# Low halves, range check and first reads of a float64 MLP's weights, moved between engines and queues

## The chip, the cores and the metric

The kernel runs on one core of a Trainium2 chip. The metric is the device time of one execution in microseconds. The kernel before took 887.0 us (median of 3 runs, 886.07 to 888.24). The execution that the profiler recorded took 887.57 us, of which 885.9 us are the span of its instructions.

Engines are named as the profile does: PE is TensorE's matmuls and PEld its weight loads, DVE is VectorE, ACT is ScalarE, POOL is GpSimd, SP is SyncE, whose queue (SPq) issues nearly all transfers.

## The reference, cut to what matters

Three stages work on 3072 tokens of 384 features. A gated linear attention (4 sequences of 768 positions, 8 heads of 48) feeds a dense MLP, and that feeds a mixture of 8 experts in which each token goes to one.

```
f = 1 / (1 + exp(-f_logit))
state = f[t] * state + outer(k[t], v[t]);  y[t] = q[t] @ state      # attention
h = x @ w_in;  x2 = (h * sigmoid(h)) @ w_out                        # first MLP: 384 -> 2048 -> 384
e = argmax(x2 @ w_gate);  out = p[e] * relu(x2 @ w1[e]) @ w2[e]     # 8 experts: 384 -> 1024 -> 384
```

The MLP's two matrices arrive as float64 (8 bytes a value), everything else as float32. So w_in and w_out are 6.3 MB each, and the kernel has to make float32 values of them before it can use them.

## The kernel before, in words

Tokens are cut into 24 chunks of 128. Chunks go through the attention in six steps (`att0` to `att5`), and through the MLP in 9 groups of 2 or 3 chunks. For each group and each of the 16 tiles of 128 hidden features there is a slot: `moe_h` makes the tile's hidden values (`ph` in PSUM), ACT takes a tanh (`se`), DVE multiplies (`sg`), ACT rounds that to a high half (`gh`), and a subtraction gives the low half (`gl`). `moe_o` of that tile comes two slots later (LAG = 2) and adds to the group's output (`px`). Every product is three matmuls: high by high, high by low, low by high. The 144 slots go: group 0 tiles 0 to 7 (slots 0 to 7), group 1 all 16 tiles (slots 8 to 23), group 0 tiles 8 to 15 (slots 24 to 31), and then group by group, with 384 columns in place of 256. After the last slot come the experts.

The weights of the MLP are made in 32 pieces of 384 KB (16 of w_in, 16 of w_out), each needed from its tile's slot on in group 1, half of them already in group 0. For a piece, SP reads the raw words into a buffer (`in_raw`, `out_raw`; pool `raw`, 2 buffers; a w_in piece takes two transfers, a w_out piece one). `narrow` then makes float32 bits of them with three DVE instructions: a TENSOR_SCALAR (line 288) and two SCALAR_TENSOR_TENSOR (lines 291 and 294) into `in_cv` or `out_cv`. A fourth DVE instruction, the TENSOR_REDUCE of line 249, takes the least magnitude of the raw high words into `wmin`; at the end of the run that decides whether a slower, general version must follow. ACT then rounds to the high half (`in_hi`, `out_hi`, line 225), and POOL subtracts (`in_lo`, `out_lo`, line 226). Instructions that are pinned in program order are shown at a helper's line, 198.

Which instruction follows which is laid down when the program is built. A table gives each step a slot, a scheduler may move instructions on an engine as far as their data allow, and the order of TensorE's matmuls and of what is pinned stays as written. On the chip each engine takes its list in order, and an instruction that waits holds up all behind it. The transfers of a queue also start in order, and a new one must find one of 8 completion semaphores free.

Other names that the rows show: `kt` and `qt` are the turned keys and queries of a chunk (`att2`), `am` the masked scores, `a_all` the chunk's decay (written to DRAM as `ends` and read back), `state` the running state, `xs` the table of 4096 rows from which the experts read, filled first with a constant by 8 transfers of 776 KB (`prefill`, from a row in the tile `big`).

Of the kernel before, what the change touches and what calls it, by code (L numbers as in the profile page):

```python
# [9 lines left out]
F32 = mybir.dt.float32  # L10
# [11 lines left out]
P = 128  # L22
CAP = 512
ROW = 388
# [11 lines left out]
STP = (1, 2, 3, 4, 5, 6, 7)  # L36
PI = 12
PO = 12
CX = 0
LF = -27  # L40
LV = -16
CL = 32
ND = 1
MO = 'oeh'
TAIL = 'TooflfmfpfrffwgfkfftF'
# [9 lines left out]
ST6 = (14, 17, 19, 21, 23, 25)  # L55
LD = (-30, -30, -10, -5, -3, 5, 11)
LFD = ()
WP = ()
S1 = (-2, 1, 3, 5, 6, 8)
ASH = 3  # L60
SG = 2
# [14 lines left out]
PRD = 2  # L76
PU = 1
PD = 2
LOV = (8, 8)
FMIN = -44.0  # L80
LMIN = -43.9
ST = ST0, ST1, ST2, ST3, ST4, ST5, ST6
# [9 lines left out]
def kernel(  # L92
# [14 lines left out]
    nc = tc.nc  # L107
    B, H, S, D = q.shape
    NT, DM = out.shape
    DFF = moe_w_in.shape[1]  # L110
    E, _, F2 = moe2_w1.shape
    KC = DM // P
    NF = DFF // P
# [18 lines left out]
    main = ExitStack()  # L132
    ps = main.enter_context(tc.tile_pool(name="ps", bufs=1, space=PSUM))
    wts = main.enter_context(tc.tile_pool(name="wts", bufs=16))
    raw = main.enter_context(tc.tile_pool(name="raw", bufs=2))
    phase = ExitStack()
    att = phase.enter_context(tc.tile_pool(name="att", bufs=1))
    late = phase.enter_context(tc.tile_pool(name="late", bufs=1))
# [21 lines left out]
    wgc = const.tile([P, KC, E], F32, name="wgc")  # L160
    big = late.tile([P, 6 * 512], F32R, tag="big", name="big")
    xt0 = [big[:, i * 2 * DM : (i + 1) * 2 * DM].rearrange("p (r c t) -> p r c t", r=2, c=KC) for i in range(2)]
    extra = [big[:, 4 * DM + ROW + i * DM : 4 * DM + ROW + (i + 1) * DM].bitcast(U32) for i in range(2)]
    zrow = big[:, 4 * DM : 4 * DM + ROW].bitcast(F32)
    BANKS = {0: "haahhaaa", 1: "haahhaaa"}

# [30 lines left out]
    def keep(fn):  # L197
        return lambda *a, **k: tc.keep_in_program_order(fn(*a, **k))

    def new_unit(key):  # L200
        kind = key[0]
        full = [P, 4, KC, P] if kind in ("in", "w1") else [P, 4, DM]
        nm = "_".join(str(x) for x in key)
        units[key] = tuple(wts.tile(full, F32R, tag="wt", name=f"{nm}_{x}") for x in ("hi", "lo"))

    def part_of(src, kind, i, n):
        cols = slice(i * P, (i + n) * P)
        return (src[:, cols] if kind in ("in", "w1") else src[cols, :]).rearrange("(c p) f -> p c f", p=P)

    def load_raw(t, src, kind, i):  # L210
        cols = slice(i * P, (i + 1) * P)
        if kind == "out":
            view = lambda a: a[cols, :]
        else:
            view = lambda a: a[:, cols]
        x = view(src).bitcast(U32)
        if kind == "out":
            nc.sync.dma_start(out=t, in_=x.rearrange("(c p) f -> p c f", p=P))
            return
        nc.sync.dma_start(out=t[:96], in_=x[: KC * 96].rearrange("(c p) f -> p c f", c=KC))  # L220
        nc.sync.dma_start(out=t[96:], in_=x[KC * 96 :].rearrange("(c p) f -> p c f", c=KC))

    def split(key, h, x, lo_engine):
        hi, lo = units[key]
        (keep(nc.scalar.copy) if key == ("w1", 1, 1) and RT > 1 else nc.scalar.copy)(hi[:, h], x)  # L225
        lo_engine.tensor_sub(lo[:, h], x, hi[:, h].bitcast(F32))  # L226

    def load_piece(kind, i):
        u, h = divmod(i, 4)
        src = moe_w_in if kind == "in" else moe_w_out  # L230
        nm = f"{kind}_{i}"
        if h == 0:
            new_unit((kind, u))
        shape = [P, KC, P] if kind == "in" else [P, 1, DM]
        if src.dtype == I64:
            t = raw.tile(shape + [2], U32, tag="raw", name=f"{nm}_raw")
            load_raw(t.rearrange("p c f w -> p c (f w)"), src, kind, i)
            made = len(pieces_made)
            pieces_made.append(i)
            if made % (2 + CX) < CX and made < CL:  # L240
                x = extra[made % (2 + CX)]
                x = x.rearrange("p (c f) -> p c f", c=shape[1])
            else:
                x = raw.tile([P, ROW], U32, tag="cv", name=f"{nm}_cv", bufs=2)[:, :DM].rearrange("p (c f) -> p c f", c=shape[1])
            t2 = t.rearrange("p c f w -> p (c f) w")
            pin = keep if i < (PI if kind == "in" else PO) else lambda fn: fn
            narrow(t2, x.rearrange("p c f -> p (c f)"), pin)
            j = i if kind == "in" else NF + i
            pin((nc.gpsimd if made in WP else nc.vector).tensor_reduce)(
                out=wmin[:, j : j + 1], in_=t2[:, :, 1].bitcast(F32), axis=AX.X, op=ALU.min, apply_absolute_value=True  # L250
            )
            x = x.bitcast(F32)
        else:
            x = raw.tile(shape, F32, tag="raw", name=f"{nm}_raw")
            nc.sync.dma_start(out=x, in_=part_of(src, kind, i, 1))
        split((kind, u), h, x if kind == "in" else x[:, 0], nc.gpsimd)

    pieces_made = []
    halves = {}
# [91 lines left out]
    def att2(n):  # L351
        pq = use(n, 1, f"pq_{n}")
        for r in range(NPR):
            pe.transpose(
                pq[:112, r * P : (r + 1) * P],
                qpads[n % 2][:, 2 * r : 2 * r + 2, :].rearrange("p h d -> p (h d)")[:, :112],
                ident,
            )
        pk = use(n, 2, f"pk_{n}")
        for r in range(NPR):  # L360
            pe.transpose(
                pk[:112, r * P : (r + 1) * P],
                kpads[n % 2][:, 2 * r : 2 * r + 2, :].rearrange("p h d -> p (h d)")[:, :112],
                ident,
            )
        pq3 = pq[:112, :].rearrange("p (r t) -> p r t", r=NPR)
        pk3 = pk[:112, :].rearrange("p (r t) -> p r t", r=NPR)
        kt = att.tile([112, NPR, P], F32, tag="kt", name=f"kt_{n}", bufs=2)
        qt = att.tile([112, NPR, P], F32, tag="qt", name=f"qt_{n}", bufs=2)
        nc.scalar.copy(qt, pq3)  # L370
        nc.vector.tensor_copy(kt, pk3)
        bd[n] = (kt, qt)

    def att3(n):
# [117 lines left out]
    def moe_g(g, i):  # L492
# [4 lines left out]
        (nc.scalar.copy if g < GACT else nc.vector.tensor_copy)(hi, t)  # L497
        (nc.gpsimd if (g, i) < LOV else nc.vector).tensor_sub(lo, t, hi.bitcast(F32))  # L498
        gt[g, i] = (hi, lo)
# [554 lines left out]
    wmin = const.tile([P, 32], F32, name="wmin")  # L1054
# [28 lines left out]
    def at(slot, fn, *args):  # L1083
        plan.setdefault(slot, []).append((fn, args))
# [24 lines left out]
    for u in range(4):  # L1109
        for h in range(4):  # L1110
            at(UI[4 * u + h], load_piece, "in", 4 * u + h)
            at(UO[4 * u + h], load_piece, "out", 4 * u + h)
    for g in range(NG - 1):
        s0 = {0: L0, 1: L1}.get(g, pos[g, NF - 1] + LAG + 1)
        for t in range(sizes[g]):
            at(s0 + t, flip_rows, g, t)
            at_end(s0 + t, gate, g, t)
        s0 += sizes[g]
        at(s0, pick, g)
        at(s0 + RD, route, g)  # L1120
# [119 lines left out]
```

## Time and profile before

| | |
|---|---|
| median of 3 runs | 887.0 us |
| profiled execution | 887.57 us, span 885.9 us |
| PE busy | 837.0 us (94%) |
| DVE busy | 432.1 us (49%) |
| ACT busy | 380.6 us (43%) |
| POOL busy | 344.5 us (39%) |
| PE's wait behind an instruction of another engine, 0 to 150 us | at most 7.7 us for one cause |

How to read it: a windows row gives for a stretch the busy time of each engine with the count of instructions, then the mean clock granted to TensorE (1.00 is 2.4 GHz, 0.50 is 1.2 GHz), the busy share of the 16 DMA engines (the records of packets overlap, so it can come out above 1), and GB/s. In the timeline the bracket is the engine's idle time before the instruction and what ended it.

### The profile page before, as it was taken

How to read it: one execution, taken by the hardware profiler on the slowest of the kernel's cores; microseconds unless marked ns; L12 is line 12 of the kernel's file. 1: busy time of each engine (PE TensorE's matmuls, PEld its weight loads, DVE VectorE, ACT ScalarE, POOL GpSimd, SP SyncE). 2: the span in 40 equal slices, each digit the busy share in tenths (PEclk: the TensorE clock that was granted, in tenths of full speed). 3: DMA queues.
4: the chain of work that ended last, by engine and by line, in shares of the span. 5: the costliest groups of instructions: out<-in, count | busy, mean ns of one | idle time of the engine just before them, and what ended most of it. 6: DMA issues, size and time to landing. Idle time of an engine off the chain costs nothing. (4 is left out here: it accounts for less than half of the span.)

```text
span 885.9 us, 15549 instructions
## 1 busy us (share of the span) xinstructions
PE 837.0 (94%) x5684; PEld 796.0 (90%) x5684; DVE 432.1 (49%) x1040; ACT 380.6 (43%) x796; POOL 344.5 (39%) x361
## 2 busy tenths in 40 slices
PE   7779888999999999999999999999999999999994
PEld 4678778998999999999999999998898999999994
DVE  5889876355444345344335434333545355345520
ACT  5443443435345445345345343354444354345420
POOL 6565745443535525544544533445500100110011
PEclk9769979999999999999999999999899999999998
DMA  9654539231122313213212310213246344445500
GB/s 157 148 134 121 139 115 305 65 64 37 58 43 55 80 21 63 65 35 60 69 32 44 75 24 19 72 37 117 92 142 197 130 127 153 136 131 186 161 28 27
DMA packets 157479, 83.38 MB, mean 94 GB/s; under 512 B 114924, under 2 KB 153053, under 8 KB 157392
## 3 DMA queue, kind: packets, MB, share of 16 engines
q1 hardware_dynamic: 154112, 72.79, 31.7%
q0 software_dynamic: 3280, 9.49, 2.9%
q8 instruction: 47, 0.77, 0.4%
q14 instruction: 40, 0.33, 0.1%
HBM read 63.03 MB, written 16.33 MB: 90 GB/s over the span
## 5 line engine op out<-in xcount | busy, mean ns | idle before, releaser
L498 POOL TENSOR_TENSOR gl<-sg,gh 128x384 fp32r<-128x384 f32 (+1 forms) x136 | 133.2, 980 | 193.7 <-ACT gh L497 191.4
L489 DVE SCALAR_TENSOR_TENSOR sg<-se,ph 128x384 f32<-128x384 f32 (+1 forms) x144 | 73.0, 507 | 205.6 <-ACT se L487 193.0
L323 PE MATMUL px<-out_lo,gh 128*128 128x384 f32 x384 | 138.1, 360 | 1.0 <-ACT x L532 0.8
L487 ACT ACTIVATE se<-ph 128x384 f32<-128x384 f32 (+1 forms) x144 | 65.2, 453 | 167.9 <-PE ph L323 158.5
L323 PE MATMUL px<-out_hi,gl 128*128 128x384 f32 x384 | 132.1, 344 | 5.2 <-POOL gl L498 5.1
L323 PE MATMUL px<-out_hi,gh 128*128 128x384 f32 x384 | 131.4, 342 | 0.0
L323 PE MATMUL ph<-xtl,in_hi 128*128 128x384 f32 (+1 forms) x384 | 128.1, 334 | 1.2 <-POOL xtl L461 0.6
L323 PE MATMUL ph<-xth,in_hi 128*128 128x384 f32 (+1 forms) x384 | 125.5, 327 | 0.0
L323 PE MATMUL ph<-xth,in_lo 128*128 128x384 f32 (+1 forms) x384 | 125.4, 327 | 0.0
L497 ACT CAST gh<-sg 128x384 fp32r<-128x384 f32 (+1 forms) x144 | 68.6, 476 | 72.6 <-DVE sg L489 71.2
L766 POOL DMA_INDIRECT out_dram<-o,oi x25 | 24.1, 962 | 178.7 <-DVE w_lo L226 112.4
L225 ACT CAST w_hi<-w_raw 128x384 fp32r<-128x384 f32 x124 | 57.4, 512 | 56.6 <-DMA w_raw<-in_moe_w_dram 54.7
L323 PEld LDWEIGHTS px<-out_hi,gl 128*128 128x128 f32 x384 | 73.8, 192 | 6.7 <-POOL gl L498 6.0
L323 PEld LDWEIGHTS ph<-xtl,in_hi 128*128 128x128 f32 x384 | 73.9, 193 | 3.8 <-POOL xtl L461 2.5
L323 PEld LDWEIGHTS px<-out_lo,gh 128*128 128x128 f32 x384 | 73.5, 192 | 3.7 <-ACT x L532 1.1
L323 PEld LDWEIGHTS ph<-xth,in_lo 128*128 128x128 f32 x384 | 74.1, 193 | 0.0
L323 PEld LDWEIGHTS ph<-xth,in_hi 128*128 128x128 f32 x384 | 73.9, 192 | 0.0
L323 PEld LDWEIGHTS px<-out_hi,gh 128*128 128x128 f32 x384 | 73.6, 192 | 0.0
L226 DVE TENSOR_TENSOR w_lo<-w_raw,w_hi 128x384 fp32r<-128x384 f32 x104 | 53.5, 554 | 35.9 <-ACT w_hi L225 35.6
L323 PE MATMUL po<-w_lo,hh 128*128 128x384 f32 (+6 forms) x200 | 67.8, 339 | 0.0
L323 PE MATMUL po<-w_hi,hh 128*128 128x384 f32 (+6 forms) x200 | 67.3, 336 | 0.0
L323 PE MATMUL po<-w_hi,hl 128*128 128x384 f32 (+6 forms) x200 | 67.3, 336 | 0.0
(240 smaller groups left out, 1692.6 us busy)
## 6 DMA issues: line engine op xcount, KB each, us to landing
w_raw<-in_moe_w_dram SPq DMA_DIRECT2D x64, 384.0 KB
xs<-big SPq DMA_DIRECT2D x8, 776.0 KB
out_raw<-in_moe_w_out_dram SPq DMA_DIRECT2D x16, 384.0 KB
xe<-xs SPq DMA_DIRECT2D x7, 776.0 KB
f<-in_f_logit_dram SPq DMA_DIRECT2D x24, 192.0 KB
k<-in_k_dram SPq DMA_DIRECT2D x24, 192.0 KB
q<-in_q_dram SPq DMA_DIRECT2D x24, 192.0 KB
v<-in_v_dram SPq DMA_DIRECT2D x24, 192.0 KB
```

Source lines behind the costliest of these rows:

```text
L225: (keep(nc.scalar.copy) if key == ("w1", 1, 1) and RT > 1 else nc.scalar.copy)(hi[:, h], x)
L226: lo_engine.tensor_sub(lo[:, h], x, hi[:, h].bitcast(F32))
L323: ins = nc.tensor.matmul(*a, **k)
L487: nc.scalar.activation(e, ph[:, :GT], AF.Tanh, scale=0.5)
L489: nc.vector.scalar_tensor_tensor(out=t, in0=e, scalar=1.0, in1=ph[:, :GT], op0=ALU.add, op1=ALU.mult)
L497: (nc.scalar.copy if g < GACT else nc.vector.tensor_copy)(hi, t)
L498: (nc.gpsimd if (g, i) < LOV else nc.vector).tensor_sub(lo, t, hi.bitcast(F32))
L766: nc.gpsimd.indirect_dma_start(out=out[:, :], out_offset=bass.IndirectOffsetOnAxis(ap=idx[:n], axis=0), in_=o[:n], in_offset=None, bounds_ ...
```

## The change

For the MLP's float64 weights:

- the low half is subtracted on DVE in place of POOL (32 instructions);
- the range check no longer stands with the piece. Each piece is read from DRAM a second time (`verify_piece`, tiles `in_again`, `out_again`), and DVE's TENSOR_REDUCE works on that copy. The table places these from slot 44 on, one every 2.5 slots;
- the pool of raw buffers has 4 buffers, which second reads share;
- the first 4 pieces (5 transfers) are read from ACT's queue, the others from SP's.

Two more edits: the copy of the turned keys (`kt`) of chunks 0 to 6 goes from DVE to ACT, and the low half of the hidden values (`gl`) is made on POOL for groups 0 and 1 alone (32 instructions); for the 104 of groups 2 to 8 that POOL made, it goes to DVE.

```
-LOV = (8, 8)
+LOV = (2, 0)
+RAW = 4
+VS = 44
+VD = 5
+KACT = 7
-    raw = main.enter_context(tc.tile_pool(name="raw", bufs=2))
+    raw = main.enter_context(tc.tile_pool(name="raw", bufs=4))
...
-            load_raw(t.rearrange("p c f w -> p c (f w)"), src, kind, i)
...
+            load_raw(t.rearrange("p c f w -> p c (f w)"), src, kind, i, nc.scalar if made < RAW else nc.sync)
...
-            j = i if kind == "in" else NF + i
-            pin((nc.gpsimd if made in WP else nc.vector).tensor_reduce)(
-                out=wmin[:, j : j + 1], in_=t2[:, :, 1].bitcast(F32), axis=AX.X, op=ALU.min, apply_absolute_value=True
-            )
...
-        split((kind, u), h, x if kind == "in" else x[:, 0], nc.gpsimd)
+        split((kind, u), h, x if kind == "in" else x[:, 0], nc.vector)
+
+    def verify_piece(kind, i):
+        src = moe_w_in if kind == "in" else moe_w_out
+        if src.dtype != I64:
+            return
+        shape = [P, KC, P] if kind == "in" else [P, 1, DM]
+        t = raw.tile(shape + [2], U32, tag="raw", name=f"{kind}_{i}_again")
+        load_raw(t.rearrange("p c f w -> p c (f w)"), src, kind, i, nc.sync)
+        j = i if kind == "in" else NF + i
+        nc.vector.tensor_reduce(
+            out=wmin[:, j : j + 1], in_=t.rearrange("p c f w -> p (c f) w")[:, :, 1].bitcast(F32), axis=AX.X,
+            op=ALU.min, apply_absolute_value=True,
+        )
...
-        nc.vector.tensor_copy(kt, pk3)
+        (nc.scalar.copy if n < KACT else nc.vector.tensor_copy)(kt, pk3)
...
+    for j in range(2 * NF):
+        at(VS + j * VD // 2, verify_piece, ("in", "out")[j % 2], j // 2)
```

The order of TensorE's instructions is the same in both programs. Two places differ in a way that matters below. The first is SP's queue at the end of the weights' reads. In a name such as `out_13_raw`, 13 is the tile; `v_6`, `q_7`, `k_7` and `ends` belong to chunks 6 and 7. Before:

```order
L218 DMA out_13_raw_1374<-in_moe_w_out_dram 128x768
L218 DMA out_14_raw_1430<-in_moe_w_out_dram 128x768
L344 DMA ends_75<-ep_6_1420 1x384
L192 DMA k_7_1709<-in_k_dram 128x8x48
L192 DMA q_7_1707<-in_q_dram 128x8x48
L346 DMA a_all_84<-ends_75 48x4x1 x2
L218 DMA out_15_raw_1469<-in_moe_w_out_dram 128x768
L1134 DMA xs_76<-big_91 128x4x388 x8
L192 DMA v_7_1740<-in_v_dram 128x8x48
```

And now, at the same place of SP's queue:

```order
L1141 DMA xs_76<-big_91 128x4x388 x8
L218 DMA out_13_raw_1345<-in_moe_w_out_dram 128x768
L192 DMA v_6_1176<-in_v_dram 128x8x48
L218 DMA out_14_raw_1400<-in_moe_w_out_dram 128x768
L218 DMA out_15_raw_1438<-in_moe_w_out_dram 128x768
L220 DMA in_0_again_2523<-in_moe_w_in_dram 96x3x256
L221 DMA in_0_again_2523<-in_moe_w_in_dram 32x3x256
L349 DMA ends_75<-ep_6_1390 1x384
L192 DMA q_7_1675<-in_q_dram 128x8x48
L192 DMA k_7_1677<-in_k_dram 128x8x48
L218 DMA out_0_again_2666<-in_moe_w_out_dram 128x768
L351 DMA a_all_84<-ends_75 48x4x1 x2
```

The 8 transfers of the prefill stood behind the last piece of weights; they now stand ahead of the last three pieces, of `v_6` and of chunk 6's `ends`, and the second reads follow.

The second place is DVE's list from slot 21 on (`sg_1_13` is group 1, tile 13, slot 21; `sg_0_8` is slot 24). Before:

```order
L489 SCALAR_TENSOR_TENSOR sg_1_13_1562<-se_1_13_1560,ph_1_13_1550 128x256
L390 TENSOR_TENSOR am_6_0_1574<-sc_6_0_1564,trir_78 128x512
L390 TENSOR_TENSOR am_6_1_1576<-sc_6_1_1565,trir_78 128x512
L489 SCALAR_TENSOR_TENSOR sg_1_14_1600<-se_1_14_1598,ph_1_14_1588 128x256
L489 SCALAR_TENSOR_TENSOR sg_1_15_1624<-se_1_15_1622,ph_1_15_1612 128x256
L446 TENSOR_TENSOR state_85<-pu_6_1638,a_all_84 48x4x48 x2
L489 SCALAR_TENSOR_TENSOR sg_0_8_1671<-se_0_8_1669,ph_0_8_1659 128x256
```

And now, the first part of the same place:

```order
L494 SCALAR_TENSOR_TENSOR sg_1_13_1530<-se_1_13_1528,ph_1_13_1518 128x256
L395 TENSOR_TENSOR am_6_0_1542<-sc_6_0_1532,trir_78 128x512
L395 TENSOR_TENSOR am_6_1_1544<-sc_6_1_1533,trir_78 128x512
L293 TENSOR_SCALAR out_13_cv_1347<-out_13_raw_1345 128x384
L296 SCALAR_TENSOR_TENSOR out_13_cv_1347<-out_13_raw_1345,out_13_cv_1347 128x384
L494 SCALAR_TENSOR_TENSOR sg_1_14_1568<-se_1_14_1566,ph_1_14_1556 128x256
```

And further on, from the first of the second reads to slot 25's product (`sg_0_9`):

```order
L258 TENSOR_REDUCE wmin_96<-in_0_again_2523 128x1
L299 SCALAR_TENSOR_TENSOR out_15_cv_1440<-out_15_raw_1438,out_15_cv_1440 128x384
L226 TENSOR_TENSOR out_3_lo_1273<-out_14_cv_1402,out_3_hi_1272 128x384
L226 TENSOR_TENSOR out_3_lo_1273<-out_15_cv_1440,out_3_hi_1272 128x384
L494 SCALAR_TENSOR_TENSOR sg_0_8_1639<-se_0_8_1637,ph_0_8_1627 128x256
L258 TENSOR_REDUCE wmin_96<-out_0_again_2666 128x1
L451 TENSOR_TENSOR state_85<-pu_6_1606,a_all_84 48x4x48 x2
L494 SCALAR_TENSOR_TENSOR sg_0_9_1663<-se_0_9_1661,ph_0_9_1651 128x256
```

The narrowing of tile 13 of w_out now stands between the products of slots 21 and 22, and reduces of second reads stand among the products from slot 24 on. Although the table places them from slot 44, 28 of the 32 stand ahead of slot 36's product (`sg` of group 2, tile 4), and the other 4 ahead of slot 39's.

## Rows read from the trace of the kernel before

**Rows 1.** Windows by stretch: us, busy by engine (count), TensorE clock, DMA share, GB/s.
```profile
20.00:40.00 20.00, 14.03 (x104) 12.00 (x101) 17.14 (x30) 7.45 (x15) 13.35 (x11) 0.78 0.66 156
40.00:60.00 20.00, 14.92 (x76) 13.93 (x75) 17.27 (x29) 11.09 (x19) 10.32 (x11) 0.59 0.40 113
...
80.00:100.00 20.00, 19.04 (x159) 17.83 (x158) 17.77 (x38) 8.82 (x23) 13.06 (x16) 1.00 0.51 136
...
300.00:400.00 100.00, 99.22 (x756) 95.38 (x752) 43.88 (x110) 43.13 (x84) 43.98 (x41) 1.00 0.23 49
```
**Rows 2.** Waits of TensorE, 0 to 150: us in total, times, longest.
```profile
PE pq L328 <- DVE qpad L343: 7.7, 3, 3.9
...
PE ph L323 <- POOL in_lo L226: 3.1, 1, 3.1
```
**Rows 3.** Windows, 14 to 145: all; L226; tile wmin; L291; L294; tile kt.
```profile
14.00:145.00 131.00, 107.55 (x733) 99.67 (x733) 114.08 (x203) 59.43 (x128) 79.98 (x78) 0.80 0.55 141
...
14.00:145.00 131.00, 0.00 (x0) 34.92 (x32) 0.80 0.55 141
...
14.00:145.00 131.00, 17.38 (x32) 0.00 (x0) 0.80 0.55 141
...
14.00:145.00 131.00, 24.46 (x32) 0.80 0.55 141
...
14.00:145.00 131.00, 22.48 (x32) 0.80 0.55 141
...
14.00:145.00 131.00, 8.13 (x112) 6.82 (x112) 4.08 (x6) 0.80 0.55 141
```
**Rows 4.** Lines L294 and L198's reduce, 14 to 145: ns min/median/max, first and last start.
```profile
L294 DVE SCALAR_TENSOR_TENSOR out_cv<-out_raw,out_cv x16: 543/762/1240, 17.8 to 142.7; 128x384 uint32<-128x384 uint32 x16
...
L198 DVE TENSOR_REDUCE wmin<-out_raw x12: 539/541/546, 18.2 to 112.8; 128x1 f32<-128x384 f32 x12
```
**Rows 5.** Groups of VectorE by form, 14 to 145: busy, mean ns, idle before.
```profile
L198 DVE TENSOR_SCALAR out_cv<-out_raw 128x384 uint32<-128x384 uint32 x12 | 9.0, 753 | 0.8 <-DMA out_raw<-in_moe_w_out_dram 0.8
...
L198 DVE TENSOR_SCALAR in_cv<-in_raw 128x384 uint32<-128x384 uint32 x12 | 8.3, 694 | 2.3 <-DMA in_raw<-in_moe_w_in_dram 1.4 <-POOL in_lo L226 0.9
```
**Rows 6.** Timeline of VectorE: start, us, what, [idle before <- releaser].
```profile
36.79 0.42 DVE L489 SCALAR_TENSOR_TENSOR sg<-se,ph 128x256 f32<-128x256 f32 x1 [1.81 <-ACT se L487]
...
41.56 0.35 DVE L198 TENSOR_SCALAR in_cv<-in_raw 128x384 uint32<-128x384 uint32 x1
...
116.46 0.42 DVE L489 SCALAR_TENSOR_TENSOR sg<-se,ph 128x256 f32<-128x256 f32 x1 [0.81 <-ACT se L487]
...
125.54 0.36 DVE L288 TENSOR_SCALAR out_cv<-out_raw 128x384 uint32<-128x384 uint32 x1 [2.21 <-DMA out_raw<-in_moe_w_out_dram]
...
152.98 0.42 DVE L489 SCALAR_TENSOR_TENSOR sg<-se,ph 128x256 f32<-128x256 f32 x1 [2.11 <-ACT se L487]
...
187.55 0.55 DVE L489 SCALAR_TENSOR_TENSOR sg<-se,ph 128x384 f32<-128x384 f32 x1
```
**Rows 7.** Page, parts 5 and 6: low halves of the late weights; prefill of the slots.
```profile
L226 DVE TENSOR_TENSOR w_lo<-w_raw,w_hi 128x384 fp32r<-128x384 f32 x104 | 53.5, 554 | 35.9 <-ACT w_hi L225 35.6
...
xs<-big SPq DMA_DIRECT2D x8, 776.0 KB
```
**Rows 8.** Windows: small loads at the start; one w_in read; the prefill.
```profile
0.00:5.00 5.00, 2.74 (x6) 0.73 (x6) 2.24 (x4) 1.32 (x2) 4.34 (x30) 1.00 0.65 125
...
118.00:120.00 2.00, 2.00 (x9) 1.90 (x9) 2.00 (x4) 0.00 (x0) 1.13 (x2) 0.50 0.61 195
...
146.00:148.00 2.00, 2.00 (x18) 2.00 (x16) 0.42 (x1) 0.68 (x3) 0.76 (x2) 1.00 1.05 367
```
**Rows 9.** Timeline of SyncE's queue: reads of the raw weights.
```profile
110.42 0.33 SPq L220 DMA_DIRECT2D in_raw<-in_moe_w_in_dram  x1
...
122.30 0.35 SPq L218 DMA_DIRECT2D out_raw<-in_moe_w_out_dram  x1
...
127.45 4.98 SPq L218 DMA_DIRECT2D out_raw<-in_moe_w_out_dram  x2
```

More of the change, by code (lines that the diff above doesn't have):

```diff
@@ L38 @@
 PO = 12
-CX = 0
 LF = -27
 LV = -16
-CL = 32
+KACT = 7
 ND = 1
@@ L57 @@
 LFD = ()
-WP = ()
 S1 = (-2, 1, 3, 5, 6, 8)
@@ L162 @@
     xt0 = [big[:, i * 2 * DM : (i + 1) * 2 * DM].rearrange("p (r c t) -> p r c t", r=2, c=KC) for i in range(2)]
-    extra = [big[:, 4 * DM + ROW + i * DM : 4 * DM + ROW + (i + 1) * DM].bitcast(U32) for i in range(2)]
     zrow = big[:, 4 * DM : 4 * DM + ROW].bitcast(F32)
@@ L208, in part_of, with load_raw @@
         return (src[:, cols] if kind in ("in", "w1") else src[cols, :]).rearrange("(c p) f -> p c f", p=P)
-    def load_raw(t, src, kind, i):
+    def load_raw(t, src, kind, i, eng):
         cols = slice(i * P, (i + 1) * P)
@@ L217, in load_raw @@
         if kind == "out":
-            nc.sync.dma_start(out=t, in_=x.rearrange("(c p) f -> p c f", p=P))
+            eng.dma_start(out=t, in_=x.rearrange("(c p) f -> p c f", p=P))
             return
-        nc.sync.dma_start(out=t[:96], in_=x[: KC * 96].rearrange("(c p) f -> p c f", c=KC))
-        nc.sync.dma_start(out=t[96:], in_=x[KC * 96 :].rearrange("(c p) f -> p c f", c=KC))
+        eng.dma_start(out=t[:96], in_=x[: KC * 96].rearrange("(c p) f -> p c f", c=KC))
+        eng.dma_start(out=t[96:], in_=x[KC * 96 :].rearrange("(c p) f -> p c f", c=KC))
     def split(key, h, x, lo_engine):
@@ L236, in load_piece @@
             t = raw.tile(shape + [2], U32, tag="raw", name=f"{nm}_raw")
-            load_raw(t.rearrange("p c f w -> p c (f w)"), src, kind, i)
             made = len(pieces_made)
             pieces_made.append(i)
[L240 to L244, printed above, removed]
+            load_raw(t.rearrange("p c f w -> p c (f w)"), src, kind, i, nc.scalar if made < RAW else nc.sync)
+            x = raw.tile([P, ROW], U32, tag="cv", name=f"{nm}_cv", bufs=2)[:, :DM].rearrange("p (c f) -> p c f", c=shape[1])
             t2 = t.rearrange("p c f w -> p (c f) w")
```

## The prediction

> **What bounds the kernel now.** I read the windows first. In mid-run PE hardly rests (99.22 of 100 us in 300 to 400, at full clock), and since PE's order doesn't change, little can be won there. The start is different: in 20 to 40 PE is busy 14.03 of 20 us, in 40 to 60 14.92 at a granted clock of 0.59, while DVE is busy 17.14 and 17.27 [rows 1]. PE's waits name DVE (7.7 us for `pq` behind `qpad`) and, once, POOL's low half of a weight (3.1 us) [rows 2]. Over 14 to 145 us, when all 32 pieces are made, DVE is busy 114.08 of 131 us, and the clock is 0.80 [rows 3]. So DVE's list sets the pace until slot 22, and what the change is worth is what it takes off that list, less what it queues in front of it. One stretch is an exception: in 80 to 100 PE is busy 19.04 of 20 us at full clock [rows 1], so DVE's relief gains next to nothing there.
>
> My marks are the products `sg` of slots 0, 16, 24 and 36, at 36.79, 116.46, 152.98 and 187.55 us [rows 6].
>
> **The change part by part, slots 0 to 16.** The reduces are off the list: 32, 17.38 us [rows 3]. The six copies `kt` in the stretch are off: 4.08 us [rows 3]; ACT, busy 59.43 of 131 us, takes them. The 32 low halves come on. Late in the run, where DVE makes the same subtraction, one takes 554 ns [rows 7]: 32 x 0.554 = +17.7 us. POOL loses 34.92 of its 79.98 us [rows 3].
>
> That relief matters because DVE's instructions stretch. The last step of the narrowing takes between 543 and 1240 ns, the reduce always 539 to 546 [rows 4]; the first step takes 0.35 us at its shortest [rows 6] and 753 and 694 on average [rows 5]. Against the shortest, the two long steps lose 24.46 + 22.48 - 64 x 0.543 = 12.2 us [rows 3, 4], the first step 17.3 - 24 x 0.35 = 8.9 us in the 24 counted [rows 5, 6]. I put this down to POOL working at the same time: with 44% of POOL's work gone, 44% of 21.1 us = 9.3 us come back. The new subtractions are exposed like the long steps (12.2 / 64 = 0.19 us each, at 56% of POOL's work): 32 x 0.11 = +3.4 us. The Trainium skill has the same in GPSIMD Engine Reference, § Key points: GpSimd shares its SBUF interfaces with VectorE, and and the contention is with VectorE's instructions that run in a two-port mode or have two SBUF inputs, which a reduce at plain speed is not. By this rule a reduce that is immune was traded for a subtraction that isn't, so the gain would be 9.3 less 3.4; without it, nothing stretches by POOL and nothing comes back.
>
> Sum on DVE: -17.4 - 4.1 + 17.7 - 9.3 + 3.4 = -9.7 us. To this come two kinds of waits. Four buffers let reads run ahead: the narrowing's waits for reads, 0.8 and 1.4 us at the first step of pinned pieces [rows 5], go, and such single waits as the 2.21 us at 125.54 [rows 6]; say -4. Against that, a subtraction on DVE waits for ACT's rounding of the same piece with DVE's list behind it, which POOL took on itself. The narrowing of another piece often stands between, so I take 0.2 us of 32 times, +6 us; the bounds are 0 and 32 x 0.54 = 17 (as long as a step of the narrowing each time) [rows 4]. ACT's five transfers stand among its first instructions, and the fourth piece's must wait for a semaphore of the first piece's read, with the first rounding of `f` behind it: +1 us, bounds 0 and 5. The sum is -6.7 us: slot 16 at some 109.5 instead of 116.46. Bounds -13.7 (no wait for ACT, no delay at the start) and +12.3 (no gain from the buffers, both delays in full).
>
> **Slots 16 to 24.** The prefill now starts when POOL's memset of its row has passed, right behind slot 15's `gl`, so at about slot 16: 110 us. It is 8 x 776 KB = 6.36 MB [rows 7] at 367 GB/s with every DMA engine busy [rows 8]: 17.4 us, to 127.5. Behind it stand tiles 13 to 15 of w_out. A w_in read of 393 kB took 0.61 of a 2 us window [rows 8], so 1.2 us is the floor for one: 131.5 with `v_6`. DVE waits for tile 13 with slot 22's product behind it, and slot 24's product stands behind tiles 14 and 15 and the first reduce: 0.35 + 2 x 0.54 for a narrowing, 0.5 for ACT's rounding, 0.55 for the subtraction, and as much again for what stands between, some 4 us [rows 4, 6]. Slot 24 comes at 135.5 against 152.98. Then the `ends` of chunk 6, behind the prefill too, must land before `a_all` is read, and DVE's `state` stands in front of slot 25's product: some 4 us from slot 24 to 25, to about 140.
>
> **Slots 24 to 36.** 28 reduces stand in this stretch, so 28 reads of 393 kB must land, with about six loads of q, k and v at some 1.0 us each (125 GB/s at a share of 0.65, 197 kB) [rows 8]. Floor from 131.5: 28 x 1.2 + 6 = 39.6, to 171. With two buffers, the reads ran from 110.42 to 127.45 in five steps, 3.4 us a piece; with four, half of that would be 1.7 [rows 9]: 54 us, to 185. A buffer is held shorter now (3.24 us from the issue at 122.30 to the first use at 125.54, and a reduce of 0.54) [rows 4, 6, 9], which by four is under the floor of 1.2. I take 1.4: 45 us, 177, and 3 us for SP's own waits (its list has loads that wait for DVE, POOL and PE between the reads): slot 36 at 180 against 187.55. So some 10 of 17 us go back here.
>
> **After slot 36.** 104 low halves go from POOL to DVE, 104 x 0.554 = 58 us on an engine that was busy 43.88 of 100 us [rows 1]. Their cover is the two slots between a tile's hidden values and its use. If DVE's list runs late this cover goes; I take 0, bounds -2 and +8.
>
> Sum: -7.5 us on the profiled 887.57, and that run was 0.6 above the median: **880 us**, own range 875 to 884.
>
> **Rivals.** *The reads hide.* DMA keeps 1.2 us a piece, PE runs slots 25 to 36 as fast as before (about 33 us from 140): slot 36 at 173, 14.5 us gained, 873 us. For it: the engines' share of 0.23 in mid-run [rows 1]; against it: floor and need are equal, with no slack for SP's waits. *DVE's list stands behind its reads.* A reduce waits for a read; the products behind it wait; ACT, POOL and PE then release q, k, v and `ends` late, SP's list stops at those, and the next reads are late. If only two reads are in flight, one costs (3.24 + 0.54) / 2 = 1.9 us: 28 x 1.9 + 6 = 59, slot 36 at 191, and with PE at half clock after each stop 893 us. It decides from 1.78 us a piece on, (187.55 - 131.5 - 6) / 28. It would also show PE at half clock, as in 40 to 60 [rows 1]. For it: the prefill ahead of the last pieces, and 3.4 us a piece with two buffers. *No change.* The first four pieces, 4 x 1.2 = 4.8 us of all DMA engines, are read while q, k and f of the first chunks come in; if those come later by that much, and the subtraction's waits reach 8 us, -7.5 + 3.8 + 2 = -1.7 on 887.6 is 886 us. The share of 0.65 in the first 5 us [rows 8] leaves room for a third of these reads. The Trainium skill has the rule in DMA: Bandwidth & Descriptors, § Issuing engines are not separate DMA queues: transfers of all queues interleave on the same 16 engines, so a second queue saves only time at issue. By that rule the second queue brings nothing and this case stands; by the share alone it is a third of it.
>
> **How the numbers follow.** Forecast 0.40, reads hide 0.20, list behind its reads 0.24, no change 0.16. A difference below 0.3% (2.7 us) can't be told from none. Faster: 0.40 + 0.20 = 0.60; same 0.16; slower 0.24. The range reaches to 870 (the reads hide, with 3 us more at the start) and to 894 (the third case).
>
> **What would show it.** Right: shorter narrowing steps on DVE, some 104 us of DVE work in place of 114 up to slot 22, slot 16 near 110 us, slot 24 near 136, slot 36 near 180, DVE's longest waits for `out_raw` of tile 13 and for second reads. Wrong: slot 16 at 116 or later (the subtraction's waits, or POOL isn't why DVE stretches); the prefill not starting near 110; reads at under 1.3 us or over 1.8 us each; PE waiting for `gl` in mid-run by more than the few us of now.

## The result: 879.4 us, and how the profile after stands to the one before

The changed kernel takes 879.37 us in the median of 5 executions (877.70 to 882.08), the kernel before 887.0 (886.07 to 889.39 in the 5 beside it): a ratio of 0.9915, 95% interval [0.9888, 0.9941]. That is the 880 us of the forecast. But the 7.5 us did not come together in the way it says, and two of its steps were wrong in opposite directions.

The profiled execution of the changed kernel is the slowest of its five (882.08 us, span 880.4), so its lead over the kernel before (span 885.9) is 5.5 us, not 7.6. The page's first part, engine by engine:

```profile
PE 829.3 (94%) x5684; PEld 788.7 (90%) x5684; DVE 484.2 (55%) x1169; ACT 381.4 (43%) x803; POOL 206.2 (23%) x225
```

Windows that answer to [rows 1], and those from 120 to 200 us (columns as there: us, busy of PE, PEld, DVE, ACT and POOL with counts, clock, DMA share, GB/s):

```profile
20.00:40.00 20.00, 14.66 (x138) 12.85 (x137) 18.18 (x34) 9.97 (x23) 7.53 (x6) 0.83 0.83 174
...
120.00:140.00 20.00, 20.00 (x165) 19.64 (x164) 11.92 (x26) 9.08 (x23) 7.81 (x9) 0.98 1.02 274
140.00:160.00 20.00, 18.45 (x124) 17.29 (x123) 11.73 (x30) 7.05 (x19) 5.86 (x8) 1.00 0.97 239
160.00:180.00 20.00, 17.71 (x134) 15.90 (x133) 12.72 (x25) 4.54 (x12) 1.99 (x3) 1.00 1.02 245
180.00:200.00 20.00, 17.00 (x93) 16.14 (x93) 13.16 (x34) 6.69 (x16) 7.08 (x6) 0.83 0.92 204
...
300.00:400.00 100.00, 100.00 (x751) 97.09 (x750) 56.75 (x133) 44.23 (x87) 21.36 (x19) 1.00 0.24 49
```

The reader is to see three things. From 120 to 140 PE is busy without a gap: it is the bound there. From 140 to 200 it rests for 6.8 us in all, its clock falls to 0.83 at the end, and the DMA share stays between 0.92 and 1.02. And in 300 to 400 VectorE has gone from 43.88 [rows 1] to 56.75 us, GpSimd from 43.98 to 21.36.

The marks of [rows 6] in the changed kernel (timeline of VectorE: start, us, what, idle before and its releaser), for slots 0, 16, 24 and 36:

```profile
40.24 0.42 DVE L494 SCALAR_TENSOR_TENSOR sg<-se,ph 128x256 f32<-128x256 f32 x1 [0.87 <-ACT se L492]
...
108.65 0.42 DVE L494 SCALAR_TENSOR_TENSOR sg<-se,ph 128x256 f32<-128x256 f32 x1 [2.04 <-ACT se L492]
...
141.04 0.42 DVE L494 SCALAR_TENSOR_TENSOR sg<-se,ph 128x256 f32<-128x256 f32 x1
...
186.80 0.54 DVE L494 SCALAR_TENSOR_TENSOR sg<-se,ph 128x384 f32<-128x384 f32 x1
```

Slot 16 is 7.8 us ahead of before, slot 24 11.9, slot 36 only 0.75: nearly all that was won by slot 24 is gone twelve slots later, and the 5.5 us of the end are won after that. A finer scale is PE's own list, whose order didn't change. I take the start of the first product `px` of each tile from PE's timeline; mark n is the product for slot n's tile, which PE runs two slots later. Lead over the kernel before, in us (minus is earlier); the first column is before:

```
mark   before  changed  no 2nd reads  in place  gl on GpSimd  gl alone
  0      51.5    +0.9       +1.5        +2.3        +2.3        +0.2
  8      92.9    -5.3       -4.7        -3.6        -3.6        +0.9
 16     129.5    -6.6       -6.1        -6.1        -4.4        +1.5
 18     139.9   -11.8      -11.4       -11.3        -9.7        +2.5
 22     152.2   -11.7      -11.6       -11.4        -9.6        +2.3
 28     165.6    -9.7      -11.5       -11.2        -8.1        +2.3
 34     187.0    -5.8      -11.5       -11.2        -1.4        +2.3
 35     192.0    +0.5      -11.5       -11.3        +3.5        +2.3
 46     244.1    -0.9      -13.0       -14.2        +3.3        +1.1
 78     381.0    -2.4      -14.6       -14.9        +2.7        -0.5
110     517.8    -3.6      -15.4       -14.3        +2.4        -1.7
134     603.2    -5.5      -17.3       -16.2        +2.4        -3.6
142     620.3    -4.9      -16.4       -14.6        +3.2        -2.7
```

The other columns belong to the experiments. Each is one profiled execution; at mark 0, where four of these kernels have the same lists, they differ by 1.4 us, so a difference of 2 us in one column is no finding. What an edit is worth rests on the ratios.

**Where it goes between mark 22 and 35.** The chain of waits in the changed kernel, 130 to 200 us (start, us, what), runs through the second reads:

```profile
139.18 5.46 DMA in_again<-in_moe_w_in_dram
144.74 0.56 DVE wmin L258
145.32 0.31 SPq L220
145.68 6.86 DMA in_again<-in_moe_w_in_dram
152.64 0.56 DVE wmin L258
...
179.78 5.05 DMA in_again<-in_moe_w_in_dram
184.93 0.55 DVE wmin L258
185.48 0.89 DVE qpad L348
...
186.80 0.55 DVE sg L494
```

One buffer's turn is a read of 5 to 7 us, a reduce and the next issue: 6 to 8 us, in which four buffers bring four pieces. The 28 reduces ahead of slot 36 start from 138.98 to 186.33 us, 1.75 us apart on average. Behind each reduce stand the products and masks that PE needs, and behind these ScalarE (26.3 us of waits for `sg`, 7.7 us in the kernel below with its reads in place) and the router. The waits of all engines, 140 to 205 us (us in total, times, longest):

```profile
ACT gh L502 <- DVE sg L494: 26.3, 12, 5.2
...
DVE wmin L258 <- DMA in_again<-in_moe_w_in_dram: 10.8, 12, 2.6
...
PE plt L328 <- ACT rt L574: 4.6, 2, 3.0
```

**Where it comes from after mark 38.** PE's weight loads in the kernel before, 200 to 610 us, waited for GpSimd seven times (a view that [rows 2] did not reach):

```profile
PEld px L323 <- POOL gl L498: 2.8, 2, 1.9
PEld ph L323 <- POOL xtl L461: 2.5, 5, 0.9
```

In the changed kernel the longest rows of the same answer are these, and GpSimd is in none:

```profile
PEld sc L328 <- issue: 3.7, 15, 0.2
PEld plt L328 <- ACT rt L574: 3.2, 2, 1.9
```

2.8 + 2.5 = 5.3 us, and the marks gain 5.5 us from 38 to 134, in eight steps of 0.33 to 1.87 us. `xtl`, the low half of a token tile, stayed on GpSimd; the waits for it went too, with GpSimd's load.

### The profile page after: what moved, and what is told of

Same layout as the page of the kernel before. It is cut to its first block, busy times and chain, and to the rows that moved or that the text cites. A ratio compares the mean times of both kernels' runs of the same rounds, so it can differ in the third digit from the quotient of the medians.

```text
span 880.4 us, 15470 instructions
## 1 busy us (share of the span) xinstructions
PE 829.3 (94%) x5684; PEld 788.7 (90%) x5684; DVE 484.2 (55%) x1169; ACT 381.4 (43%) x803; POOL 206.2 (23%) x225
## 4 chain that ended last, share of the span: by engine, by line
PE 65%; DMA 14%; issue 8%; DVE 6%; ACT 3%; SPq 2%; POOL 1%; POOLq 0%; DVEq 0%; ACTq 0%
PE px L328 19%; PE ph L328 19%; PE po L328 6%; PE p L328 5%; DMA out_dram<-o,oi 5%; PE py L328 4%; DMA in_again<-in_moe_w_in_dram 4%; PE sc L328 2%; DMA w_raw<-in_moe_w_dram 2%; DMA f<-in_f_logit_dram 2%; PE plt L328 1%; DMA out_again<-in_moe_w_out_dram 1%; PE p_r L328 1%; PE pk L333 1%; PE pl L328 1%
## 5 line engine op out<-in xcount | busy, mean ns | idle before, releaser
L503 DVE TENSOR_TENSOR gl<-sg,gh 128x384 fp32r<-128x384 f32 (+1 forms) x112 | 72.3, 646 | 45.2 <-ACT gh L502 44.7
L322 POOL TENSOR_TENSOR lfl<-f,lfh 128x384 fp32r<-128x384 f32 x24 | 24.5, 1020 | 200.2 <-DVE lfh L321 174.3
```

The costliest lines, as they stand in the source:

```text
L322: (nc.vector if n in LFD else nc.gpsimd).tensor_sub(lo, f2, hi.bitcast(F32))
```

## The experiments

All ratios are against the kernel before, run beside them on the same chip, with 95% intervals.

**No second reads.** The range check of the weights is left out.

```
-        at(VS + j * VD // 2, verify_piece, ("in", "out")[j % 2], j // 2)
+        pass
```

> The changed kernel without the 32 second reads and their reduces (the range check of the weights is left out). Theory: in slots 24 to 36 the second reads, bunched there, cost what was won before: the first product px of slot 22 lies 11.8 us ahead of the kernel before and that of slot 35 0.5 us behind it. Without them that lead stays: px mark 35 some 9 to 12 us earlier than in the changed kernel, time 867 to 870 us. Rival: the lead is lost anyway (VectorE's list, now with gl of the groups from 2 on, or a transfer that was late before too); then mark 35 stays within 3 us of 192 and the time is 876 to 880.

871.06 us, 0.98 [0.9771, 0.9829], against 0.9915 with the reads. The lead of 11.5 us at mark 22 stays to mark 35, as the theory says; the rival falls. The 871.06 us are a little above the 867 to 870 that I gave. And the lead does not grow either between marks 18 and 34, with nothing left to wait for: PE is the bound there.

**Reads held in their place.** The table has the reads from slot 44, but nothing held them there.

```
-        nc.vector.tensor_reduce(
+        keep(nc.vector.tensor_reduce)(
             out=wmin[:, j : j + 1], ...
```

> The changed kernel with its reduces held in program order, so that they and the reads behind them stand where the table puts them, one to two or three slots, from slot 45 to 122. Theory: only the bunching costs (28 reads at some 1.7 us each with DMA full, 0.97 to 1.02 of the engines); spread over 77 slots they cost at most 0.5 us of VectorE each where it has room: within 1.5 us of the kernel without second reads, 867 to 871. Rival: each read costs its time wherever it stands (a reduce stops VectorE's list until its data is there): 876 to 882, with PE waiting for gl or x in mid-run.

869.89 us, 0.9778 [0.9757, 0.9799]: not to be told from no reads at all. The same 32 reads and reduces cost 1.2 to 1.4%, 10 to 12 us, bunched, and nothing that can be told when spread. Windows of this kernel, where the bunch was:

```profile
140.00:160.00 20.00, 20.00 (x142) 19.78 (x141) 8.02 (x23) 9.22 (x23) 8.19 (x10) 1.00 0.34 80
160.00:180.00 20.00, 20.00 (x156) 19.36 (x155) 10.97 (x21) 7.49 (x16) 3.95 (x5) 1.00 0.22 44
```

PE is full, and the DMA share is 0.34 and 0.22 in place of 0.97 and 1.02. From 140 to 200 us PE rests for 1.6 us in place of 6.8.

**Low halves `gl` back on GpSimd**, and **`gl` on VectorE alone** (the kernel before with this one edit).

```
-LOV = (2, 0)
+LOV = (8, 8)
```
```
-LOV = (8, 8)
+LOV = (2, 0)
```

> The changed kernel with the 104 low halves gl of groups 2 to 8 back on GpSimd. Theory: what the changed kernel wins after slot 38 (its px marks go from 0.0 to 5.5 us ahead, in steps of 0.35 to 1.9 us at places where PE waited for GpSimd's xtl or gl) is GpSimd's relief from gl, so it goes: 4 to 5.5 us slower than the changed kernel, 883 to 885, with PE waits for gl or xtl of GpSimd at the same places. Rival: the late gain has another source (PE's clock, an accident of one execution): 878 to 881.

> The kernel before with one edit: the 104 low halves gl of groups 2 to 8 on VectorE. Theory: the late gain alone, 5 us, and nothing before slot 24: 881 to 883, px mark 35 within 1 us of before, the end 4 to 5.5 us earlier. Rival: 886 to 888.

On GpSimd: 890.49 us, 1.0025 [1.0007, 1.0043], a little slower than before. Alone: 883.2 us, 0.9937 [0.9916, 0.9958], and it goes from 1.9 us behind at mark 38 to 3.6 ahead at 134, 5.5 us, in steps at the same marks, with no wait of the weight loads for GpSimd left from 200 to 610 us. So the late gain is `gl`. With `gl` back on GpSimd the loads wait for it again, 200 to 610 us:

```profile
PEld px L328 <- POOL gl L503: 3.2, 3, 1.9
PEld ph L328 <- POOL xtl L466: 2.5, 5, 0.9
```

The theory gave 4 to 5.5 us for it; the ratios differ by 1.1%, some 10 us. Between the two profiled executions, 890.4 - 880.4 us of span, the marks show 2.1 us at mark 22 already, where both have the same lists, 0.9 from there to mark 35, 4.9 from 35 to 134 as expected, and 2 after that. What the part beyond the 5 us is, stays open.

**Low halves of the weights back on GpSimd.** This and the next two undo one part of the kernel with its reads in place, so that the bunch doesn't hide what they do.

```
-        split((kind, u), h, x if kind == "in" else x[:, 0], nc.vector)
+        split((kind, u), h, x if kind == "in" else x[:, 0], nc.gpsimd)
```

> The kernel with its reads held in place, with one part undone: the 32 low halves of the weights back on GpSimd. Theory (GpSimd stretches VectorE): the narrowing's two long steps, whose median fell from 762 to 870 ns (w_out, before) to 552 to 554, go back to 700 ns or more, though no reduce stands beside them; VectorE's work to slot 22 falls by no more than 17.7 - 9 = 9 us. By the sum of the prediction taken backwards (17.7 off, 9.3 back on, 3.4 and the 3.7 us of waits for ScalarE off) product px of slot 16 comes some 15 us earlier, unless PE, busy at 20 of 20 us from 120 us on, leaves no room: then 866 to 869. Rival one (four buffers or the missing reduces, not GpSimd, shortened the steps): they stay at 550 ns, and the gain is as large or larger. Rival two: GpSimd's own list is the bound, PE waits for in_lo and out_lo as it did once in the kernel before (3.1 us), and the time is 872 to 878.

881.25 us, 0.992 [0.9889, 0.9952], against 0.9778: 1.4% slower, where the sum of the prediction, taken backwards, gives a faster kernel. Here are first the groups of VectorE and GpSimd in this kernel by form, 14 to 130 us (busy, mean ns, idle before), then those of the kernel with its reads in place:

```profile
L226 POOL TENSOR_TENSOR in_lo<-in_cv,in_hi 128x384 fp32r<-128x384 f32 x16 | 17.5, 1093 | 14.6 <-ACT in_hi L225 14.2 <-PE px L328 0.3
...
L299 DVE SCALAR_TENSOR_TENSOR in_cv<-in_raw,in_cv 128x384 uint32<-128x384 uint32 x16 | 15.5, 970 | 0.4
L299 DVE SCALAR_TENSOR_TENSOR out_cv<-out_raw,out_cv 128x384 uint32<-128x384 uint32 x15 | 13.7, 915 | 0.3
L296 DVE SCALAR_TENSOR_TENSOR in_cv<-in_raw,in_cv 128x384 uint32<-128x384 uint32 x16 | 12.6, 788 | 0.3
L296 DVE SCALAR_TENSOR_TENSOR out_cv<-out_raw,out_cv 128x384 uint32<-128x384 uint32 x15 | 12.1, 804 | 0.4
L198 DVE TENSOR_SCALAR in_cv<-in_raw 128x384 uint32<-128x384 uint32 x12 | 10.7, 894 | 0.3 <-POOL out_lo L226 0.3
```
```profile
L226 DVE TENSOR_TENSOR in_lo<-in_cv,in_hi 128x384 fp32r<-128x384 f32 x16 | 10.7, 678 | 1.6 <-ACT in_hi L225 1.5
L226 DVE TENSOR_TENSOR out_lo<-out_cv,out_hi 128x384 fp32r<-128x384 f32 x13 | 9.9, 766 | 2.2 <-ACT out_hi L225 1.9
L296 DVE SCALAR_TENSOR_TENSOR in_cv<-in_raw,in_cv 128x384 uint32<-128x384 uint32 x16 | 9.7, 609 | 0.1
L299 DVE SCALAR_TENSOR_TENSOR out_cv<-out_raw,out_cv 128x384 uint32<-128x384 uint32 x13 | 9.4, 726 | 0.2
L296 DVE SCALAR_TENSOR_TENSOR out_cv<-out_raw,out_cv 128x384 uint32<-128x384 uint32 x13 | 8.7, 669 | 0.2
L299 DVE SCALAR_TENSOR_TENSOR in_cv<-in_raw,in_cv 128x384 uint32<-128x384 uint32 x16 | 8.7, 551 | 0.2
L198 DVE TENSOR_SCALAR in_cv<-in_raw 128x384 uint32<-128x384 uint32 x12 | 6.4, 533 | 0.0
```

The two long steps take 15.5 + 13.7 + 12.6 + 12.1 = 53.9 us for 31 pieces with the low halves on GpSimd, 1.74 us a piece, and 36.5 us for 29, 1.26 a piece, without. VectorE is busy longer in the same stretch although its subtractions, 20.6 us for 29 pieces, are gone. The windows 14 to 130 of the one and the other:

```profile
14.00:130.00 116.00, 91.38 (x669) 84.23 (x668) 98.33 (x153) 57.60 (x122) 73.42 (x70) 0.82 0.60 144
```
```profile
14.00:130.00 116.00, 97.81 (x716) 90.71 (x715) 94.75 (x183) 61.84 (x133) 43.54 (x46) 0.85 0.71 181
```

So GpSimd's work does stretch VectorE's (rival one falls), and by more than I reckoned: what VectorE saves by giving 32 subtractions away it pays back in the narrowing. The medians of the theory came back in part only. The last step of w_in has 1108 ns, that of w_out 559, and the means of all four long steps rose.

The theory's gain failed with this: product `px` of slot 16 was to come some 15 us earlier and came 6.4 us later than with the reads in place, and the time was to be 866 to 869 us. Paying back explains that nothing is won. It does not explain all of the 12 us lost, and two other things differ. Slot 16's `sg` stands at 115.5 us in place of 110.3. And GpSimd's list, which also fills the prefill's row, is behind: the prefill is issued at 131.40 us in place of 109.19, so more pieces come in ahead of it, and 18 steps of the narrowing stand between the products of slots 16 and 17 in place of 12; these lie 15.3 us apart in place of 12.0. PE's waits up to 150 us name VectorE (7.8 us for `pq` behind `qpad`, 2.2 with the reads in place), not GpSimd's low halves; rival two gave a range that misses the time by 3 us, by another mechanism.

**First reads from SyncE's queue.**

```
-RAW = 4
+RAW = 0
```

> The kernel with its reads held in place, with one part undone: the first four weight reads from SyncE's queue. Theory: the reads from ScalarE's queue come in beside q, k and f and delay the start: first product sg of slot 0 stood at 40.2 instead of 36.8 us. Undone, f's second load lands near 5 us instead of 9, and sg of slot 0 comes 2 to 4 us earlier; but the first tiles of the weights come later, and by slot 6 the difference is gone: within 1.5 us in the end, 868.5 to 871. Rival: the 3 us stay to the end, 866 to 867; or the first weights then come so late that slots 2 to 8 lose their lead (px mark 2 is 4 to 5.6 us ahead), 873 to 875.

868.07 us, 0.977 [0.9736, 0.9803]; with them on ScalarE's queue 0.9778: no difference that can be told, and a time between the ranges of theory and rival. Its marks lie 4.4 us earlier at mark 0, 3.2 at mark 8 and 1.8 at mark 36: the start does gain and the gain shrinks, but more slowly than the theory has it (gone by slot 6). The `sg` of slot 0 did not move (41.51 and 41.44 us), where the theory gave 2 to 4 us; three instructions more stand ahead of it in VectorE's list, two steps of a narrowing and a mask.

**Copies `kt` back on VectorE.**

```
-KACT = 7
+KACT = 0
```

> The kernel with its reads held in place, with one part undone: kt of chunks 0 to 6 back on VectorE. Theory: 4.1 us on the engine that sets the pace of slots 0 to 16: px marks of slots 8 to 17 3 to 5 us later, kept to the end, since PE has no rest from slot 18 on: 873 to 875. Rival: these copies stand in VectorE's idle moments (it is busy 95 of 116 us) and cost nothing: 869 to 871.

878.16 us, 0.9872 [0.9836, 0.9909], against 0.9778: 0.9%, some 8 us for the 4.1 us that these six copies take. Theory and rival are both too small; the lead at mark 8 goes from -3.6 to +1.7 and at mark 36 from -11.2 to -5.0. Where the second 4 us come from is not shown.

**Four buffers alone**, in the kernel before.

```
-    raw = main.enter_context(tc.tile_pool(name="raw", bufs=2))
+    raw = main.enter_context(tc.tile_pool(name="raw", bufs=4))
```

> The kernel before with one edit: four staging buffers instead of two. Theory: VectorE's waits for reads in the stretch of the weights (0.8 + 1.4 + 2.2 + 2.0 us in the kernel before) go, some 4 us at px mark 16: 883 to 885. Rival: VectorE is late anyway and takes the time back: 887 to 889.

893.86 us, 1.0065 [1.0043, 1.0088]: slower, on the wrong side of both expectations. The loss is there from the start and stays: 5.7 us at mark 0, 5.4 at mark 36, 5.6 at mark 142. The timeline of VectorE in this kernel, ahead of slot 0's product, shows why: it stands at 45.55, not at 36.79 [rows 6], with 13 instructions more ahead of it than before, narrowings and reduces of pieces that are not due yet. The last of them:

```profile
42.98 1.28 DVE L291 SCALAR_TENSOR_TENSOR in_cv<-in_raw,in_cv 128x384 uint32<-128x384 uint32 x1
44.18 0.35 DVE L198 TENSOR_SCALAR in_cv<-in_raw 128x384 uint32<-128x384 uint32 x1
44.45 0.54 DVE L294 SCALAR_TENSOR_TENSOR in_cv<-in_raw,in_cv 128x384 uint32<-128x384 uint32 x1
44.92 0.54 DVE L198 TENSOR_REDUCE wmin<-in_raw 128x1 f32<-128x384 f32 x1
45.55 0.42 DVE L489 SCALAR_TENSOR_TENSOR sg<-se,ph 128x256 f32<-128x256 f32 x1
```

**Two and three buffers, and the prefill later**, each in the kernel with its reads in place and the first reads from SyncE's queue (`bufs=2`, `bufs=3`, `PF = 30` in place of 4, 4 and 16).

```
-    raw = main.enter_context(tc.tile_pool(name="raw", bufs=4))
+    raw = main.enter_context(tc.tile_pool(name="raw", bufs=2))
```
```
-    raw = main.enter_context(tc.tile_pool(name="raw", bufs=4))
+    raw = main.enter_context(tc.tile_pool(name="raw", bufs=3))
```
```
-PF = 16
+PF = 30
```

> The kernel with its reads held in place and the first reads from SyncE's queue, with two staging buffers instead of four. Theory: more buffers let the weights run ahead of the attention in VectorE's list; four buffers alone put 8 reduces and 13 instructions more ahead of slot 0's product sg, which came at 45.6 instead of 36.8 us, and made the kernel before 5.8 us slower. Two buffers bring sg of slot 0 from list place 53 to 42, some 11 x 0.55 = 6 us earlier (41.4 to about 36), but tiles 13 to 15 of w_out then stand behind the prefill and their rows come from slot 21 on: what is won at slot 0 is kept to slot 20 and some of it lost there: 863 to 868. Rival (the buffers pay: reads that wait for a free buffer stop VectorE's list): px marks 4 to 16 later than with four, 869 to 874.

> The same with three staging buffers: sg of slot 0 at list place 47, so some 3 us earlier than with four; all pieces but three stand ahead of slot 20. Theory: 865 to 867. Rival: as with four, 867 to 869.

> The kernel with its reads held in place and the first reads from SyncE's queue, with the prefill of the slots 14 slots later in the table, behind all pieces and the first second reads. Theory: the early prefill takes DMA from 107 to 127 us, but PE is busy 20 of 20 us from 120 on, and the pieces behind it are used late; so it costs nothing and moving it wins nothing: 866 to 870, px marks 18 to 36 within 1.5 us. Rival (the step of the prediction: slot 24's product stands behind the last pieces, these behind the prefill): 3 us or more earlier at px mark 18 to 24, 863 to 865.

Two buffers: 886.95 us, 0.9979 [0.9954, 1.0003]. Three: 869.83 us, 0.981 [0.9773, 0.9847]. Later prefill: 876.56 us, 0.9875 [0.9842, 0.9908]. All three expectations missed, and the marks say where (lead over before; "between" is the next experiment):

```
mark   four buffers  two    three   four, later  three, between
  8        -6.8      -4.7    -8.0      -5.7          -6.9
 18       -13.3     -12.7   -16.3     -12.0         -12.6
 20       -13.4      -2.4   -16.5     -12.2         -12.8
 22       -13.1      -1.5   -10.3     -12.2         -12.8
 34       -13.0      -0.9    -9.8     -12.2         -12.8
 38       -14.5      -1.4   -11.7      -3.8         -11.1
142       -19.8      -4.3   -16.3      -8.9         -15.0
```

With two buffers seven pieces stand behind the prefill. PE then waits for the weights themselves, 125 to 165 us:

```profile
PE ph L328 <- ACT in_hi L225: 4.5, 1, 4.5
PE ph L328 <- DVE in_lo L226: 1.9, 1, 1.9
```

With three, where four pieces stand behind it, 6 us go at marks 20 to 22, with four, where three do, nothing. So the prefill ahead of the last pieces does cost, as the prediction says, and four buffers are what pays for it: they bring all but three of the 32 in first. In time two buffers are clearly slower; three and four can't be told apart (0.981 [0.9773, 0.9847] and 0.977 [0.9736, 0.9803]). With the prefill behind all pieces it is issued at 158.83 us, and the loss of 8 us comes at marks 34 to 38, with PE waiting 7.2 us for the router's `rt`:

```profile
158.83 11.19 SPq L1141 DMA_DIRECT2D xs<-big  x8
```

**Three buffers, the prefill in between.** Last, `PF = 24` with `bufs=3`:

```
-PF = 16
+PF = 24
```

> The kernel with its reads held in place, first reads from SyncE's queue and three buffers, with the prefill eight slots later in the table: behind the last piece and chunk 7's q, k and v, ahead of chunk 7's ends and chunk 8's loads. With three buffers and the early prefill px mark 18 was 16.3 us ahead of the kernel before, and 6 us of that went at marks 20 to 22, where the pieces behind the prefill were late; with the prefill 14 slots later 8 us went at marks 35 to 38, since it was issued at 158.8 us, ahead of chunk 8's loads. Theory: in between, issued near 140 us and done before 158, it costs neither: the 16 us stay, 862 to 866. Rival: the transfers of 140 to 160 (v of chunk 7, second reads) are late in turn, or the pieces' work at slots 16 to 18 was hidden only because the prefill held it back: 868 to 872.

868.09 us, 0.9774 [0.9744, 0.9804]. The prefill is issued at 137.88 us and neither loss is seen (marks 18 to 34 stay at -12.8), but mark 18 has 12.6 and not the 16.3 us of the early prefill: 14 steps of the narrowing stand between the products of slots 16 and 17 when the prefill no longer holds the reads back, 10 before, as the rival says, and the time is in its range. This kernel, the one with its first reads on SyncE and the one with its reads in place, at 868 to 870 us, can't be told apart; all three beat the changed kernel by about 1.4%.

## Why the prediction came out right, step by step

**What bounds the start** was right up to slot 17 only. From mark 18 on PE is the bound as soon as VectorE lets it: 20.00 of 20 us in 120 to 140, and a lead that stands still at -11.5 us without second reads.

**Slots 0 to 16.** Forecast -7 us, measured -7.8 at `sg` and -6.6 at px. VectorE's work from 14 us up to slot 22 is 97 us, before 114. The forecast of 104 holds all 32 pieces; in the changed kernel 5.8 us of work on the last three come after slot 22's product, which makes it 103. The parts are less good than the sum:
- GpSimd as the cause of VectorE's stretching: shown. The first step fell from 753 and 694 ns [rows 5] to 531 and 518, the two long steps from 46.94 / 32 = 1.47 [rows 3] to 1.26 us a piece: 24 x 0.2 + 32 x 0.21 = 11.5 us in the counted ones, where I had 9.3 in all. The trace of the kernel before shows it within one run: of its 64 long steps, the 28 that ran with no GpSimd instruction beside them took 540 to 560 ns, the other 36 took 541 to 1249, 874 on average; the reduces took 537 to 553 with and without company. One such pair:

```profile
110.78 1.25 DVE L291 SCALAR_TENSOR_TENSOR out_cv<-out_raw,out_cv 128x384 uint32<-128x384 uint32 x1
110.56 1.06 POOL L226 TENSOR_TENSOR out_lo<-out_cv,out_hi 128x384 fp32r<-128x384 f32 x1
```

The Trainium skill, GPSIMD Engine Reference, § Key points, says that GpSimd shares its SBUF interfaces with VectorE and contends with instructions in a two-port mode or with two SBUF inputs; the runs agree, reduces staying at 539 to 546 ns [rows 4] and a long step, with its two inputs, going up to 970 on average. The first step has one input and stretches too; whether it runs in such a mode no run shows. What I missed: with the low halves on GpSimd and no reduces, the stretch is larger than in the kernel before, 1.74 us a piece for the two long steps against 1.47. That the reduces had been harmless company for GpSimd's work is my reading of this; no run has the reduces back with all else the same.
- Low halves on VectorE: 17.7 + 3.4 = 21.1 us forecast; 10.7 + 9.9 = 20.6 us for 29 of 32 in the kernel with its reads in place, so 22.7 for all. Their waits for ScalarE: 6 us forecast, 1.5 + 1.9 measured there.
- Buffers: -4 us forecast, with bounds that did not go above 0. This step had the wrong sign for the edit alone (1.0065). In the changed kernel four buffers have another use, which I did not see: they keep the last pieces out of the prefill's way.
- Start: +1 us forecast. Mark 0 is at +0.9, but `sg` of slot 0 came 3.5 us late, and undoing this part alone brings 4.4 us at mark 0, so the term was too small. By mark 36 1.8 us are left, within what runs differ by. The second queue brought nothing: 0.9778 with it, 0.977 without. The Trainium skill (DMA: Bandwidth & Descriptors, § Issuing engines are not separate DMA queues) says that transfers of all issuing engines interleave on the same 16 DMA engines, and that a second issuer saves only the time at issue; the two ratios agree.

**Slots 16 to 24.** The step "Slot 24 comes at 135.5" failed: 141.04. I had only DMA and VectorE in it. The prefill came at 107.56 us, near the 110 forecast, and VectorE did not wait for tile 13; but eight slots of products fill PE, and PE's time for them was not in the sum. The kernel before had PE as its bound there already, in a window that [rows 1] does not have:

```profile
140.00:160.00 20.00, 20.00 (x164) 19.64 (x164) 9.22 (x23) 8.06 (x21) 7.63 (x10) 0.99 0.96 326
```

From slot 16 to 24 it took 36.5 us; the sum had 26, and the changed kernel took 32.4. The lead at slot 24 was 11.9 us, not 17.5.

**Slots 24 to 36.** "So some 10 of 17 us go back here" was right in kind: 11.2 of 11.9 us at `sg` went back. The stretch took 45.8 us, forecast 44.5. The pace was right as a sum: 28 reduces from 138.98 to 186.33 us are 27 steps of 1.75 us with all else in the queue, and my 131.5 to 180 us, with 6 us of loads and 3 us of waits in it, are 1.73 for each of 28. Its parts were not: the floor of 1.2 us from [rows 8], a share of 0.61 scaled up to 1, was too low, since at a share of 0.99 the queue moved 239 GB/s, at which 393 kB take 1.6 us. The mechanism is that of the rival "DVE's list stands behind its reads", with the clock at 0.83 in 180 to 200. Its price was not reached: its 1.78 us a piece leave out the 6 us of loads, and with them the line lies at (187.55 - 131.5) / 28 = 2.0. Slot 36 came 6.8 us later than forecast, 5.5 of it from slot 24. That the time is the forecast's all the same has one reason:

**After slot 36.** "I take 0, bounds -2 and +8" failed: -5 us. I asked only whether VectorE could bear `gl`, not who had waited for GpSimd. PE's waits after 200 us would have told, the weight loads with 5.3 us for GpSimd and the matmuls with 2.8; I read them to 150 us only. The single edit is worth 0.9937 [0.9916, 0.9958]. With `gl` left on GpSimd the rest of the change takes 890.49 us, 1.0025 [1.0007, 1.0043], outside my range and on the side of the rivals.

So the forecast is right by luck, through two errors that cancel: slot 36 was to be 7.5 us ahead and was 0.75, and the run after it was to win nothing and won 5.

## What to carry to other kernels

When work goes from one engine to another, look in all stretches for who waited for the engine that loses it, and in the row of weight loads as well as that of products. A place in a table is not a place in the queue: work meant to fill gaps must be held in order, or it may come early and all at once; here the same reads cost 1.4% or nothing. More buffers change the order of a list, not only its waits, so look at what now stands ahead of the first product that the bound engine needs.

## What the runs showed of the hardware that was not expected

A vector instruction on VectorE beside GpSimd's subtractions can take twice its time, and which one it hits depends on what stands beside what. With the low halves on GpSimd the last step of narrowing w_in went from a median of 552 to 1108 ns and the first from a mean of 533 to 894; for w_out the median of the last step (552 and 559) and the mean of the first (530 and 549) hardly moved. One of GpSimd's subtractions takes 1093 ns on average. And a DMA share near 1 is no fixed rate: 367 GB/s in the prefill [rows 8], 239 to 245 in the second reads.
